# Attention and soft mixture of experts on one core: when the expert weights are loaded during attention

## The chip, the cores and the metric

One core of a Trainium2 chip. Times are microseconds on the device, from the first to the last instruction of a run of the whole program. A run is one launch; the time of a kernel is the median of its runs.

## What is computed

All data is float32. First comes attention over 8 batches of 12 heads, 448 positions and 64 channels, with a sigmoid in place of a softmax. Its output, as 3584 rows of 768, goes through a soft mixture of 8 experts with 4 slots each.

```python
scores = scale * np.matmul(q, k.transpose(0, 1, 3, 2)) - np.log(S)
x = np.matmul(1.0 / (1.0 + np.exp(-scores)), v)      # then laid out as 3584 x 768
logits = x @ phi                                     # 3584 x 32
slot_input = softmax(logits, axis=0).T @ x           # over all rows: 32 x 768
for e in range(8):                                   # 4 slots of each expert
    h = np.maximum(slot_input[e] @ w1[e], 0.0)       # w1[e]: 768 x 1024
    slot_out[e] = h @ w2[e]                          # w2[e]: 1024 x 768
return softmax(logits, axis=1) @ slot_out
```

The softmax over rows runs over all batches, so the experts can't start before attention is done; their weights (w1 and w2, 50 MB) can be loaded before.

## The kernel before

**Attention** runs in 24 rounds (the loop over n), three to a batch (NQ = 3). A round takes four heads as two pairs, pa and pb. Its work on TensorE: the scores of both pairs (`qk_full`, L170), their products with V (`av_full`, L188), the logits of the round before (`logits`, L217), and what the 448 positions leave over beyond three blocks of 128 (`qk_mid` L181, `av_mid` L197). ScalarE takes the sigmoids (L160). VectorE brings the output of the round before out of PSUM (`evac`, L206), transposes it (`turn`, L212) and splits the queries and keys of the next round in two parts (`split_all`, L149 and L151).

**The slot job.** From the second batch on, a round also holds a share of the mixture for the batch before, bp. Three flags name the rounds: *edge* is the first round of a batch (n = 3, 6, ...), *after* the second (n = 4, 7, ... 22) and *third* the third. In an edge round the last logits come in and the running softmax begins (`softmax_a`, `softmax_b`). In the after round VectorE finishes it (`softmax_r`, `softmax_c`) and `spread` (L281) spreads the weights of the slots: a transpose on VectorE (L283), a write to a scratch buffer in DRAM (zd, L285), and four reads back, each to another quarter of the partitions (dr, L288). The slot job of TensorE (`slot_mm`, L309, 112 matmuls) reads dr; it stands in the after round behind the logits. VectorE adds its result up in the third round (L331).

**Loads.** All DMAs are issued by SyncE's queue (SP), in the order of the program text; an entry that waits holds up those behind it. At the top of a round stand the queries and keys of the next round (`load_qk`, L134, two buffers), which wait until this round's are no longer read; in an after round then the five DMAs of `spread`; then V of the next round (`load_v`, L141, two buffers); then weights (`load_unit`, L92).

**Weights** are cut into 128 units of 384 KB, 64 of w1 and 64 of w2, loaded in that order into a ring of 47 buffers (N_A, names wa) and 21 more (N_B, names wb). The first 47 have memory of their own during attention. The loop at L432 brings their number up to (n + 1) * 47 // 21 in round n: 2 units in most rounds, 3 in some, and all 47 by round 20. The 21 take over memory of attention's buffers, so their loads wait until those are read for the last time. The other 60 are loaded as buffers come free.

**After attention** come the last batch's slot job, the experts' first layer (L519), the second in two halves of the columns (L584), and the combination (L562), whose results are copied to ring buffers and stored.

Order of instructions on TensorE, SyncE, VectorE and ScalarE is that of the program text; buffers, waits and semaphores come from the tile framework.

Of the kernel before, what the change touches and what calls it, by code (L numbers as in the profile page):

```python
# [16 lines left out]
B, H, S, D = 8, 12, 448, 64  # L17
# [5 lines left out]
NQ = NPR // 2  # L23
# [4 lines left out]
N_A = 47  # L28
# [19 lines left out]
def soft_moe_attention(ctx: ExitStack, tc: tile.TileContext, qk, v, phi, w1, w2, cst, out):  # L48
# [25 lines left out]
    state = {"next": 0, "ring": 0, "wpb": None}  # L74
# [10 lines left out]
    def load_unit():  # L85
        n = state["next"]
        if n >= len(units):
            return
        state["next"] = n + 1
        u = units[n]  # L90
        t = ring_tile()[:]
        nc.sync.dma_start(t, w1[u[1:]] if u[0] == "w1" else w2[u[1:]])  # L92
        utile[u] = t
# [9 lines left out]
    def combine_d(b, cb):  # L103
        lt = lt_all[:, b].rearrange("p (j s) -> p j s", j=NBK)
        cz = small.tile([P, NBK, 1], F32, name="cz")
        nc.vector.tensor_reduce(out=cz[:], in_=lt, axis=AX.X, op=ALU.add)
        nc.vector.tensor_scalar(cz[:], cz[:], 1e-9, None, op0=ALU.add)
        nc.vector.reciprocal(cz[:], cz[:])
        nc.vector.tensor_tensor(
            out=cb.rearrange("p (j s) -> p j s", j=NBK), in0=lt, in1=cz.broadcast_to([P, NBK, NSLOT]), op=ALU.mult)  # L110
        nc.vector.transpose(lt_all[:, b], cb)
# [4 lines left out]
    with ExitStack() as actx:  # L116
# [9 lines left out]
        def bank2(i):  # L126
            return ps.tile([P, 2, 512], F32, name=f"b{i}")
# [3 lines left out]
        def load_qk(p):  # L131
            if p < NP:
                t = ldq.tile([P, QW], F32, name="qkt")
                nc.sync.dma_start(t[:], qk[p])  # L134
                qkts[p] = t

        def load_v(n):
            if n == NG:
                return
            vs[n] = lvp.tile([P, 2 * NFULL + 1, P], F32, name="v")  # L140
            nc.sync.dma_start(vs[n][:], v[n])  # L141
# [11 lines left out]
        def split_all(p):  # L153
            if p < NP:
                for i, z in ((0, 0), (0, 1), (1, 0), (1, 1)):
                    split(p, i, z)
# [6 lines left out]
        def qk_full(p):  # L163
            qs, ks = splits[p, 0], splits[p, 1]
            for c in range(NFULL):
                u = p % 2 * NFULL + c
                sc = bank2(u % 4)
                for z, y in ((0, 0), (0, 1), (1, 0)):
                    for h, r in enumerate(heads):
                        nc.tensor.matmul(  # L170
                            sc[:, h, 0:S], ks[r, z, c * P:(c + 1) * P], qs[r, y, :], start=(z + y == 0), stop=(z == 1))
                atts[p, c] = sigmoid(f"att{u % NATT}", sc)
# [31 lines left out]
        def evac(n):  # L204
            new_x(n)
            nc.vector.tensor_copy(xTs[n][:], avs[n][:, :, 0:S])  # L206

        def turn(p):
            b, hp = divmod(p, NPR)
            if hp == 0:  # L210
                ys[b] = xp.tile([P, NPR, S], F32, name="y")
            nc.vector.transpose(ys[b][:, hp, :], xTs["p", p])  # L212
# [17 lines left out]
        def logits(n, i):  # L230
            lp = bank2(i)[:, 0, :]
            logits_job(lp, (2 * n, 2 * n + 1))
            return lp
# [21 lines left out]
        def softmax_r(b):  # L255
            zt, pe = dts[b][:, 0, :], dts[b][:, 1, :]
            n = P if b == 0 else P + 1
            nc.vector.reciprocal(zt[:, 0:n], zt[:, 0:n])
            nc.vector.tensor_tensor(out=pe[:, 0:n], in0=pe[:, 0:n], in1=zt[:, 0:n], op=ALU.mult)

        def softmax_c(b):
            pe = dts[b][:, 1, :]
            if b == 0:
                nc.vector.tensor_reduce(out=mz[:, 1:2], in_=pe[:, 0:P], axis=AX.X, op=ALU.add)
            else:
                zb = small.tile([P, 1], F32, name="zb")
                nc.vector.tensor_reduce(out=zb[:], in_=pe[:, 0:P], axis=AX.X, op=ALU.add)
                nc.vector.scalar_tensor_tensor(
                    out=mz[:, 1:2], in0=mz[:, 1:2], scalar=pe[:, P:P + 1], in1=zb[:], op0=ALU.mult, op1=ALU.add)
# [6 lines left out]
        def combine_c(b):  # L276
            neg = dts[b][:, 1, 0:P]
            nc.vector.reciprocal(neg, neg)
            nc.vector.tensor_tensor(out=lt_all[:, b], in0=lt_all[:, b], in1=neg, op=ALU.mult)

        def spread(b):  # L281
            z = dts[b][:, 0, 0:P]
            nc.vector.transpose(z, dts[b][:, 1, 0:P])  # L283
            flat = bounce.tile([P, P], F32, name="zd")
            nc.sync.dma_start(flat[:], z)  # L285
            drs[b] = xp.tile([P, 4, NBK * BLK], F32, name="dr")
            for a in range(4):
                nc.sync.dma_start(drs[b][32 * a:32 * a + 32, :, :], flat[:].rearrange("(j i) n -> i j n", j=4))  # L288
# [37 lines left out]
        def slot_evac(b):  # L326
            for a in range(4):
                if b == 0:
                    nc.vector.tensor_copy(acc_of[:, a], new_of(slots[b], a))
                else:  # L330
                    nc.vector.scalar_tensor_tensor(  # L331
                        out=acc_of[:, a], in0=acc_of[:, a], scalar=dts[b][:, 1, P:P + 1], in1=new_of(slots[b], a),
                        op0=ALU.mult, op1=ALU.add)
# [80 lines left out]
        for n in range(NG):  # L414
            pa, pb = 2 * n, 2 * n + 1
            bp = n // NQ - 1
            edge, after, third = (n >= NQ and n % NQ == i for i in range(3))
            final = n == NG - 1
            load_qk(pa + 2)
            load_qk(pb + 2)  # L420
            if third:
                slot_evac(bp)
            if n > 0:
                evac(n - 1)
                for p in ((pa - 4, pa - 3) if third else ()) + (() if after else (pa - 2, pa - 1)):
                    turn(p)
            if after:
                softmax_r(bp)
                softmax_c(bp)
                spread(bp)  # L430
            load_v(n + 1)
            while state["next"] < min(N_A, (n + 1) * N_A // 21):  # L432
                load_unit()
            if third:
                combine_c(bp)
            if edge and bp > 0 or final:
                bq = bp if final else bp - 1
                combine_d(bq, dts[bq][:, 0, 0:P])
            qk_full(pa)
            split_all(pa + 2)  # L440
            qk_full(pb)
            split_all(pb + 2)
            if final:
                avs["p", pa] = bank2(2)[:, 0, :]
                av_full(pa, True, False)
                lg = bank2(0)[:, 0, 0:P]
                nc.tensor.matmul(lg, ident, lt_all[:, B - 1], start=True, stop=False)
                logits_job(lg, [NP - 4, NP - 3], first=False, last=False)
                avs["p", pb] = bank2(3)[:, 0, :]
                av_mid(n, ((False, True), (True, False)))  # L450
                xa = xp.tile([P, 2, S], F32, name="xT", bufs=2)[:, 0, :]
                xTs["p", pa] = xa
                nc.vector.tensor_copy(xa, avs["p", pa][:, 0:S])
                turn(pa)
                av_full(pb, False, True)
                logits_job(lg, [pa], first=False, last=False)
                xb = xp.tile([P, 2, S], F32, name="xT", bufs=2)[:, 0, :]
                xTs["p", pb] = xb
                nc.scalar.copy(xb[:, 256:S], avs["p", pb][:, 256:S])
                nc.vector.tensor_copy(xb[:, 0:256], avs["p", pb][:, 0:256])  # L460
                logits_job(lg, [pb], first=False)
                turn(pb)
                break
            avs[n] = bank2(2)
            for i in range(2):
                avs["p", pa + i] = avs[n][:, i, :]
            av_full(pa, True, False)
            if edge:
                lp = logits(n - 1, 0)
                logits_add(lp, bp, False)  # L470
                softmax_a(bp)
                softmax_b(bp)
            av_full(pb, True, False)
            if n > 0 and not edge:
                lp = logits(n - 1, 3 if after else 0)
                if after:
                    combine_b(bp)
                logits_add(lp, n // NQ, n % NQ == 1)
            if after:
                slot_job(bp)  # L480
            qk_mid(n + 1)
            av_mid(n, ((False, True), (False, True)))
# [179 lines left out]
```

## Time and profile before

| | |
|---|---|
| median of 3 runs | 395.81 us (393.76 to 398.99) |
| the profiled execution | 397.69 us, span 395.9 us, clock 0.98 |
| TensorE busy | 370.6 us (94%) |
| VectorE, ScalarE busy | 227.4 us, 188.1 us |
| moved by DMA | 97.52 MB, mean 246 GB/s |
| weight units loaded | 92 to wa buffers, 36 to wb buffers |

The profile is that of one execution. PE is TensorE's matmuls, PEld its weight loads, which run beside them, DVE VectorE, ACT ScalarE, and SPq the issuing of DMAs by SyncE. A row of SP's queue gives the start and the length of issuing, not of the transfer. "Idle <- X" names what ended an engine's wait. "issue" is a wait for nothing that the profile shows. Queue q1 holds the data, queues q8 and q14 hold instructions. A line of forty digits gives the busy share in tenths over forty equal slices of the time asked for.

### The profile page before, as it was taken

To read this page: it belongs to the slowest core of one execution; us is meant where nothing else is said; L and a number is where in the kernel's file an instruction comes from. 1 tells how busy PE (TensorE), PEld (TensorE's weight loads), DVE (VectorE), ACT (ScalarE), POOL (GpSimd) and SP (SyncE) were. 2 spreads that over 40 slices of the span, in tenths; PEclk is the share of its full clock that TensorE was granted. 3 is DMA by queue.
4 is the path that set the end of the run, shared out by engine and by line. 5 is a ranking of instruction groups with operands and counts; after the bars stand their busy time and mean duration, and the time that the engine had idled before them with its cause. 6 is when DMAs were issued, how large, how long until landed. Compare 5 with 4: busy or idle time off the path is not lost.

```text
span 395.9 us, 9573 instructions
## 1 busy us (share of the span) xinstructions
PE 370.6 (94%) x4000; PEld 192.9 (49%) x4000; DVE 227.4 (57%) x531; ACT 188.1 (48%) x244; POOL 3.4 (1%) x13
## 2 busy tenths in 40 slices
PE   8999999999999999989999999999989989988760
PEld 6445556554455654455554455555465544314220
DVE  3555677776787767677767778775531420330250
ACT  4656676564667556466645666663520110230240
POOL 1000000000000000000000000000020000000000
PEclk9999999999999999999999999999997999999995
DMA  6555658645665846565376558523899999999997
GB/s 215 213 191 202 220 172 285 202 168 170 252 220 145 299 154 225 165 221 210 110 237 215 189 176 284 190 101 124 304 365 351 403 400 401 390 376 406 365 301 238
DMA packets 41851, 97.52 MB, mean 246 GB/s; under 512 B 4304, under 2 KB 16208, under 8 KB 41808
## 3 DMA queue, kind: packets, MB, share of 16 engines
q1 hardware_dynamic: 41808, 96.91, 69.5%
q8 instruction: 31, 0.51, 0.5%
q14 instruction: 12, 0.10, 0.1%
HBM read 85.43 MB, written 11.47 MB: 245 GB/s over the span
## 4 chain that ended last, share of the span: by engine, by line
PE 84%; DMA 8%; DVE 2%; issue 1%; ACT 1%; SPq 1%; ACTq 0%
PE b L188 27%; PE b L170 23%; PE px L519 6%; PE b L181 6%; PE b L197 5%; PE b L309 4%; PE po L584 4%; DMA wb<-in_w_dram 4%; PE b L217 3%; PE px L562 3%; DMA out_dram<-wb 2%; DMA qkt<-in_qk_dram 1%; PE px L536 1%; DMA zd<-t 1%; PE b L376 1%
## 5 line engine op out<-in xcount | busy, mean ns | idle before, releaser
L160 ACT ACTIVATE att<-b,nbias 128x896 f32<-128x896 f32 x144 | 132.0, 1016 | 14.9 <-PE b L170 14.9
L188 PE MATMUL b<-att,v 128*64 128x448 f32 x576 | 115.3, 545 | 0.0
L170 PE MATMUL b<-qs,ks 64*128 64x448 f32 x864 | 96.3, 372 | 0.5 <-issue 0.5
L170 PEld LDWEIGHTS b<-qs,ks 64*128 64x128 f32 x864 | 77.7, 184 | 26.9 <-PE b L181 15.5
L188 PEld LDWEIGHTS b<-att,v 128*64 128x64 f32 x576 | 38.5, 136 | 61.6 <-issue 49.9
L160 ACT ACTIVATE attm<-b,nbias 128x896 f32<-128x896 f32 x24 | 24.2, 1008 | 72.1 <-PE b L181 72.1
L206 DVE COPY xT<-b 128x896 f32<-128x896 f32 x23 | 25.1, 1092 | 34.5 <-PE b L197 34.5
L151 DVE TENSOR_TENSOR qs<-qkt,qs 128x448 fp32r<-128x448 f32 x48 | 30.0, 625 | 1.7
L151 DVE TENSOR_TENSOR ks<-qkt,ks 128x384 fp32r<-128x384 f32 x48 | 26.8, 558 | 1.6
L212 DVE STREAM_TRANSPOSE y<-xT 128x448 f32<-128x448 f32 x48 | 27.3, 617 | 0.4
L181 PE MATMUL b<-qkt 64*64 64x448 f32 x192 | 24.5, 562 | 0.6 <-DMA qkt<-in_qk_dram 0.6
L197 PE MATMUL b<-attm,v 64*64 64x448 f32 x192 | 22.5, 538 | 1.8 <-issue 1.8
L149 DVE CAST qs<-qkt 128x448 fp32r<-128x448 f32 x48 | 18.2, 379 | 7.3 <-DMA qkt<-in_qk_dram 7.0
L519 PE MATMUL px<-wa,sT 128*32 128x256 f32 x282 | 19.2, 422 | 0.9 <-DVE sT L380 0.9
L567 DVE COPY wa<-px 96x768 f32<-96x768 f32 x13 | 12.2, 952 | 12.3 <-PE px L562 12.3
L562 PE MATMUL px<-st,lt_all 32*96 32x384 f32 (+1 forms) x128 | 17.0, 524 | 1.5 <-DVE st L597 0.7
L567 ACT COPY wa<-px 128x768 f32<-128x768 f32 x13 | 10.3, 800 | 16.8 <-PE px L562 16.7
L309 PE MATMUL b<-y,dr 32*32 32x192 f32 x896 | 17.8, 331 | 0.4 <-DMA dr<-zd 0.3
L217 PEld LDWEIGHTS b<-xT,phit 128*32 128x32 f32 x384 | 9.1, 109 | 17.0 <-issue 13.4
L149 DVE CAST ks<-qkt 128x384 fp32r<-128x384 f32 x47 | 16.6, 353 | 0.0
L217 PE MATMUL b<-xT,phit 128*32 128x96 f32 (+1 forms) x384 | 16.0, 266 | 0.2
L597 DVE COPY st<-px 128x384 f32<-128x384 f32 x2 | 1.1, 558 | 25.5 <-PE px L595 25.5
(132 smaller groups left out, 235.5 us busy)
## 6 DMA issues: line engine op xcount, KB each, us to landing
wa<-in_w_dram SPq DMA_DIRECT2D x92, 384.0 KB, 7.2
qkt<-in_qk_dram SPq DMA_DIRECT2D x48, 448.0 KB, 3.7
wb<-in_w_dram SPq DMA_DIRECT2D x36, 384.0 KB, 6.6
v<-in_v_dram SPq DMA_DIRECT2D x24, 448.0 KB, 5.5
out_dram<-wa SPq DMA_DIRECT2D x13, 384.0 KB, 5.1
out_dram<-wa SPq DMA_DIRECT2D x13, 288.0 KB, 5.3
dr<-zd SPq DMA_DIRECT2D x28, 64.0 KB, 2.0
out_dram<-wb SPq DMA_DIRECT2D x3, 384.0 KB, 8.1
```

The source lines that it names most:

```text
L149: copy(dst[:, 0, :], src)
L151: nc.vector.tensor_tensor(out=dst[:, 1, :], in0=src, in1=dst[:, 0, :].bitcast(F32), op=ALU.subtract)
L160: nc.scalar.activation(att[:], sc[:, :, 0:S], AF.Sigmoid, bias=nbias, scale=QSCALE)
L170: nc.tensor.matmul(sc[:, h, 0:S], ks[r, z, c * P:(c + 1) * P], qs[r, y, :], start=(z + y == 0), stop=(z == 1))
L181: nc.tensor.matmul(sc[r, h, 0:S], t[d, S + NQK:QW], t[d, 0:S], start=True, stop=True)
L188: nc.tensor.matmul(avs["p", p][r, 0:S], vs[n][:, i * (NFULL + 1) + c, r], atts[p, c][:, h, :], start=(start and c == 0), stop=(stop and c ...
L197: nc.tensor.matmul(avs["p", 2 * n + i][d, 0:S], vt[r, NFULL, d], att[r, h, :], start=start, stop=stop)
L212: nc.vector.transpose(ys[b][:, hp, :], xTs["p", p])
L217: nc.tensor.matmul(lp[32 * j:32 * j + 32, 0:TOK[j]], phi_sb[:, p % NPR, :], xTs["p", p][:, TOF[j]:TOF[j] + TOK[j]], start=(first and m == ...
L309: nc.tensor.matmul(sl[a // 2][32 * j:32 * j + 32, a % 2, 0:NPR * BLK], drs[b][32 * a:32 * a + 32, j, c * BLK:(c + 1) * BLK], y[32 * a:32 * ...
L519: nc.tensor.matmul(ph[32 * j:32 * j + 32, uu, 0:256], sT[:, 3 * kh + kc, :], utile[("w1", e, 2 * uu + j // 2, kh)][:, kc * 256:(kc + 1) * ...
L562: nc.tensor.matmul(pf[j // 2][0:TOK[j], j % 2, 0:HALF], lt_all[r, b, 0:TOK[j]], st[r, :], start=True, stop=True)
```

## The change

In each round V of the next round is now loaded straight behind the queries and keys, ahead of `spread`. And units of weights are loaded in the first round of each batch only (n = 0, 3, ... 18), up to (n // 3 + 1) * 47 // 7: 6, 7, 7, 6, 7, 7 and 7 units. All 47 are in by round 18. The order on the other engines, the buffers and their number stay.

```diff
             if after:
                 softmax_r(bp)
                 softmax_c(bp)
+            load_v(n + 1)
+            if after:
                 spread(bp)
-            load_v(n + 1)
-            while state["next"] < min(N_A, (n + 1) * N_A // 21):
+            while n % NQ == 0 and state["next"] < min(N_A, (n // NQ + 1) * N_A // (B - 1)):
                 load_unit()
             if third:
                 combine_c(bp)
```

## The prediction

> **What bounds the kernel now.** I read the page first, then busy time by stretches, the waits of TensorE, the chain of waits around the longest of them, SP's own queue, and the DMA traffic round by round. From the page, the totals, the forty slices, the instruction queue and the issue of weights:
>
> ```profile
> span 395.9 us, 9573 instructions
> PE 370.6 (94%) x4000; PEld 192.9 (49%) x4000; DVE 227.4 (57%) x531; ACT 188.1 (48%) x244; POOL 3.4 (1%) x13
> ...
> DMA  6555658645665846565376558523899999999997
> ...
> q8 instruction: 31, 0.51, 0.5%
> ...
> wa<-in_w_dram SPq DMA_DIRECT2D x92, 384.0 KB, 7.2
> ```
>
> Two stretches with different limits show in the DMA line, and the busy time by stretches (length; busy us of each engine; clock; DMA share; GB/s) gives them figures:
>
> ```profile
> 97.00:275.00 178.00, 175.41 (x1952) 94.12 (x1944) 129.77 (x318) 104.26 (x126) 0.00 (x0) 1.00 0.57 193
> 275.00:380.00 105.00, 97.27 (x1080) 45.58 (x1076) 33.78 (x70) 25.56 (x50) 2.24 (x8) 0.97 0.99 370
> ```
>
> Up to 275 us the DMA engines are 57% busy and TensorE is busy 175.4 of 178 us: attention is bound by TensorE. After it the DMA engines are 99% busy: what is left is 81 units of weights and the output, and that stretch lasts as long as its bytes. It begins when TensorE lets go of the last ring buffers; SP's queue issues the 21 units of the second ring from there:
>
> ```profile
> 274.51 22.84 SPq L92 DMA_DIRECT2D wb<-in_w_dram  x21
> ```
>
> The change leaves the bytes after 274.5 us as they are (47 units are in before it either way, by round 18 in place of 20). So a microsecond that TensorE saves or loses before 274.5 us moves the end by about a microsecond, and nothing else counts. What TensorE waited for in 0 to 290 us, all but its start and one wait of 0.6 us for the first queries:
>
> ```profile
> PE b L197 <- issue: 1.8, 1, 1.8
> ...
> PE b L170 <- issue: 0.5, 1, 0.5
> PE b L309 <- DMA dr<-zd: 0.3, 1, 0.3
> ```
>
> That is the whole stock from which a gain can come: 2.6 us, 0.7% of the span.
>
> **The two waits with no releaser.** In the chain of waits (start, length, what) the shorter one stands behind round 10's slot job and the longer just behind round 13's; the second fence is that slot job by itself, in the timeline of TensorE:
>
> ```profile
> 133.16 0.48 issue
> ...
> 166.77 0.91 PE b L181 x8
> 167.68 1.80 issue
> 169.48 0.98 PE b L197 x8
> ```
> ```profile
> 164.57 2.19 PE L309 MATMUL b<-y,dr 32*32 32x192 f32 x112
> ```
>
> TensorE waited for no engine and no DMA. The page has 31 packets on the instruction queue of some 16 KB, and TensorE runs 4000 matmuls and 4000 weight loads: 258 instructions to a packet. A round without a slot job has 92 pairs, 184 instructions in 11.0 us (143.73 to 154.73 in SP's rows below); the slot job alone has 112 pairs, 224 instructions in 2.19 us. It is the one place where TensorE runs through nearly a block of instructions in 2 us. In the DMA view of 0.2 us at 167 us, and in that of 131.3 to 131.5 us, ahead of the shorter wait, one packet stands each time:
>
> ```profile
> q8 instruction: 1, 0.02, 30.6%
> ```
> ```profile
> q8 instruction: 1, 0.02, 28.8%
> ```
>
> They begin at 167.0 and 131.4 us; TensorE goes on 2.4 and 2.2 us later. So the next block was fetched only 2.5 us after the slot job began. What was ahead of it is in SP's queue, rounds 12 (its start) and 13:
>
> ```profile
> 143.73 0.82 SPq L134 DMA_DIRECT2D qkt<-in_qk_dram  x2
> 144.66 0.37 SPq L141 DMA_DIRECT2D v<-in_v_dram  x1
> 145.07 1.40 SPq L92 DMA_DIRECT2D wa<-in_w_dram  x3
> 154.73 0.82 SPq L134 DMA_DIRECT2D qkt<-in_qk_dram  x2
> 158.64 0.33 SPq L285 DMA_DIRECT2D zd<-t  x1
> 160.19 1.75 SPq L288 DMA_DIRECT2D dr<-zd  x4
> 162.04 0.37 SPq L141 DMA_DIRECT2D v<-in_v_dram  x1
> 162.46 0.91 SPq L92 DMA_DIRECT2D wa<-in_w_dram  x2
> ```
>
> V and two units, 1.2 MB, were issued at 162.0 to 163.4 us, and were still under way at 167. I read the wait as the fetch standing behind them.
>
> **The change part by part.** *Removed from the rounds that hold a slot job (n = 4, 7, ... 19) and from those after them:* two to three units in each; and V, which stays, moves 7.3 us forward in its round (from 162.04 to just behind the queries, as in round 12, where it is issued 0.93 us after the round's first load). Then nothing is in flight when the slot job starts. If the packet begins 0.5 us after the slot job's start (chosen between 0 and the 2.5 seen), the block is there at 164.57 + 0.5 + 2.4 = 167.5, ahead of 167.68: both waits go, **-2.28 us** (1.80 + 0.48). The bounds are 0 (the packet takes its 2.5 us all the same) and -2.28.
>
> *Added to rounds 0, 3, ... 18:* a burst of 6, 7, 7, 6, 7, 7, 7 units behind queries and V. SP needs 0.45 us for each issue; nothing is queued behind them but the next round's loads, 11 us later. The bytes do not fit. Round 12's three units, in the DMA line of 143 to 155 us (0.3 us a slice), keep the engines at it until 152.6 us:
>
> ```profile
> DMA  0000077359999999897917999999996410000000
> ```
>
> Each further unit costs 1.09 us (22.84 / 21, above): four more end at 157.0. Round 13's queries are issued at 154.73 and would have begun to move near 155.6. So they are **1.4 us late**. The split of queries on VectorE would wait for them a little; it has cover, since in that round VectorE waits for TensorE afterwards:
>
> ```profile
> 129.02 0.56 DVE L226 COPY lt_all<-b 64x128 f32<-64x128 f32 x2 [1.55 <-PE b L217]
> ```
>
> I price that at nothing; without the 1.55 us of cover it would be up to 1.4 us in five rounds.
>
> *Moved:* V ahead of the slot weights' DRAM write (zd). SP passes no wait by this: V's buffer comes free with the last product of the round before, and zd waits for VectorE until 3.9 us into the round anyway (154.73 to 158.64). On the DMA engines it counts, though: zd now stands behind V. Round 21 has queries and V and no unit, and its DMA line (250 to 261 us, 0.275 us a slice) ends at 255.5, 5.4 us after its first issue at 250.05, with SP held up for 0.8 us at V; so V ends 4.6 to 5.4 us into a round:
>
> ```profile
> 250.05 0.82 SPq L134 DMA_DIRECT2D qkt<-in_qk_dram  x2
> 250.91 1.21 SPq L141 DMA_DIRECT2D v<-in_v_dram  x1
> ```
> ```profile
> DMA  0029757999999979996100000000000000000000
> ```
>
> The landing times in round 13 (154 to 167 us):
>
> ```profile
> dr<-zd SPq DMA_DIRECT2D x4, 64.0 KB, 2.0
> zd<-t SPq DMA_DIRECT2D x1, 64.0 KB, 1.5
> ```
>
> zd lands 5.45 us into the round. Behind V alone it lands 0 to 0.5 us later; with the burst's 1.4 us ahead of both, 1.0 to 1.9 us later. The four reads (dr) and the slot job follow it. Their slack: the fourth read is issued at 160.19 + 1.75 - 0.43 = 161.5 and lands at 163.5, against a slot job at 164.57, 1.06 us. Another 0.45 us is hidden, because the job starts on the first three reads. Round 22 shows this, where zd took twice as long and the job broke off after 24 of its matmuls:
>
> ```profile
> zd<-t SPq DMA_DIRECT2D x1, 64.0 KB, 3.1
> ```
> ```profile
> 270.85 0.67 PE L309 MATMUL b<-y,dr 32*32 32x192 f32 x24
> 271.83 1.74 PE L309 MATMUL b<-y,dr 32*32 32x192 f32 x88 [0.31 <-DMA dr<-zd]
> ```
>
> It ran 2.72 us for 2.19, a loss of 0.53 us for a fourth read that landed about a microsecond after the job's start. So 1.5 us of slack stand against 1.0 to 1.9 us of lateness: a loss of 0 to 0.4 us in each of the five rounds behind seven units, 0 in the two behind six. I take 0.1, **+0.5 us** together (0 to 2.0). Round 22 has no burst ahead; its 0.53 us stays (0 to 1.0).
>
> *Sum:* 395.9 - 2.28 + 0.5 = 394.1 us of span. The profiled execution took 397.69 us, 1.8 more than its span and 1.9 more than the median of 395.81; taking the same 1.8 us off the median gives **394.0 us**. The runs themselves lie between 393.76 and 398.99, so 2% (7.9 us) is about what a measurement of this kernel can tell from no change.
>
> **The rivals.** *The backlog does not hold the fetch.* Then the two waits have another cause, they stay, and only the costs come: 395.8 + 0.5 = 396.3 us. For it speaks that rounds 4, 7 and 16 load units in the same place without such a wait; against it, that both waits have a packet 2.2 to 2.4 us ahead of their end, and that the two stand at different places (L197 and L170), as the end of a block would that shifts from batch to batch. The Trainium skill (DMA: Bandwidth & Descriptors, Queues, rings and completion order) has each DMA engine take turns between its queue rows packet by packet. By that rule a fetch would pass the backlog and this rival holds; the 2.5 us at round 13 speak against it, but the trace does not record when the fetch was asked for.
>
> *The DRAM bounce becomes the bound (slower).* zd takes 1.5 us more wherever it meets other traffic, as in round 22, on top of the 1.4 us of burst: late by 2.8, less 1.5 of slack, 1.3 us in five rounds, 0.3 in round 10, 0.7 more in round 22, 7.5 together; less 2.28, it is +5.2, **401.0 us**. It decides when zd lands later than 6.95 us into its round (5.45 + 1.5). For it: the overlap above. Against: round 22's delay went with an instruction packet at that moment, not with data.
>
> *More is won.* Both waits go, no slot job is late and round 22's 0.53 us goes too, because in the runs timed such waits are longer than in the profiled one (the slowest is 3.2 us above the median): 395.8 - 2.8 = 393.0, and down to 391.5 if the timed runs had a microsecond or more of them besides.
>
> **How the numbers follow.** Forecast 0.5 (392.8 to 395.6), no hold of the fetch 0.2, the bounce 0.18, more won 0.12. The range takes the forecast, all of the first rival, the lower part of the bounce and most of the last: 391.5 to 399.5. Faster by over 2% would need 387.9 and no stock is that large: 0.03. Slower by over 2% needs 403.7, a bounce 2 us worse in every batch than I price it: 0.05. Within 2%: 0.92.
>
> **What would show it.** Right: TensorE's waits without a releaser behind rounds 10 and 13 are gone, V stands in SP's queue ahead of zd, the second ring's first unit is issued near 272.7, and DMA traffic runs without a gap from each burst into the next round. Wrong: waits of the slot job for dr in most batches with zd landing 7 us into the round (the bounce), or waits of about 2 us without a releaser in other rounds (the fetch is not held by what I say). It is also wrong if the end does not follow the first issue of the second ring.

## The result and the profile after

The changed kernel takes 397.89 us (median of 22 runs, 394.41 to 402.13), the kernel before 395.98 us (22 runs beside them): a ratio of 1.0059, with a 95% interval of 1.0036 to 1.0082. A second series gave 1.0037 (1.0001 to 1.0073). It is slower by some 2 us, where 2 us less was forecast. Medians here and below are over all runs; ratios leave out runs more than 1.5% above the fastest of their kernel. The profiled execution took 399.63 us, span 397.9.

TensorE's waits in 0 to 290 us, complete, in the changed kernel:

```profile
PE b L404 <- DVE nbias L69: 1.2, 1, 1.2
PE b L309 <- DMA dr<-zd: 0.8, 2, 0.6
```

Both waits without a releaser are gone, as forecast. In their place stand waits of the slot job (L309) for dr. The 0.8 us are only the part in which TensorE stood still; the rest shows in how long the job takes. In the timeline of TensorE it takes 3.24 us in round 4 and 2.93 us in round 7, where it took 2.19 before:

```profile
59.05 3.24 PE L309 MATMUL b<-y,dr 32*32 32x192 f32 x112 [0.20 <-DMA dr<-zd]
...
94.93 2.93 PE L309 MATMUL b<-y,dr 32*32 32x192 f32 x112
```

SP's queue at the start of rounds 12 and 13, and the second ring's first issue:

```profile
144.45 0.82 SPq L134 DMA_DIRECT2D qkt<-in_qk_dram  x2
145.37 0.38 SPq L141 DMA_DIRECT2D v<-in_v_dram  x1
145.80 3.88 SPq L92 DMA_DIRECT2D wa<-in_w_dram  x7
155.46 0.80 SPq L134 DMA_DIRECT2D qkt<-in_qk_dram  x2
156.35 0.38 SPq L141 DMA_DIRECT2D v<-in_v_dram  x1
159.37 0.33 SPq L285 DMA_DIRECT2D zd<-t  x1
162.39 2.71 SPq L288 DMA_DIRECT2D dr<-zd  x4
...
274.97 22.79 SPq L92 DMA_DIRECT2D wb<-in_w_dram  x21
```

zd is issued 3.9 us into the round as before, but lands at 162.4, 3.0 us later, where it took 1.5. The DMA view of round 13's first 10 us (0.25 us a slice; kind, count, KB, us to landing) shows what is ahead of it: the burst from the round before, queries and V fill the engines to 5.5 us, with stragglers to 6.2.

```profile
DMA  9997795689899989999885100000000181635100
...
q8 instruction: 1, 0.02, 0.7%
...
qkt<-in_qk_dram SPq DMA_DIRECT2D x2, 448.0 KB, 4.8
v<-in_v_dram SPq DMA_DIRECT2D x1, 448.0 KB, 5.8
dr<-zd SPq DMA_DIRECT2D x4, 64.0 KB, 3.1
zd<-t SPq DMA_DIRECT2D x1, 64.0 KB, 3.0
```

V, issued at 156.35, landed at 162.15, and zd 0.2 us behind it. In this round that was not all: zd was 1.5 us late, which is just the slack, but the four reads took 3.1 us in the median, where they took 2.0 before. An instruction packet was moved in the same 10 us; that it held the reads up is not shown.

Round by round, from the first load of one to the first load of the next, for round 22 to the second ring's first issue (from SP's queue; two profiles of the changed kernel):

| round | 4 | 7 | 10 | 13 | 16 | 19 | 22 | 11 | 14 |
|---|---|---|---|---|---|---|---|---|---|
| before, us | 12.98 | 12.94 | 12.94 | 12.98 | 12.95 | 12.98 | 13.50 | 11.69 | 12.82 |
| changed | 14.29 | 13.71 | 12.98 | 13.87 | 13.63 | 13.52 | 12.98 | 10.85 | 10.82 |
| changed, second | 12.98 | 16.49 | 12.95 | 14.88 | 14.03 | 12.99 | 12.98 | 10.80 | 10.82 |
| zd to landing, changed | 4.57 | 3.51 | 2.54 | 3.00 | 3.27 | 3.43 | 3.08 | | |
| zd to landing, second | 3.04 | 4.97 | 2.41 | 3.62 | 3.45 | 2.68 | 3.14 | | |

So 4.2 us were lost in rounds 4 to 19 in the first profile and 6.6 in the second, and 3.4 us won in rounds 11, 14 and 22 (11.69 + 12.82 + 13.50 less 10.85 + 10.82 + 12.98). Round 10, behind six units, lost nothing.

### The profile page after: what moved, and what is told of

It reads as the page before. It is cut to its first block, busy times and chain, and to the rows that moved or that the text cites. A ratio compares the mean times of both kernels' runs of the same rounds, so it can differ in the third digit from the quotient of the medians.

```text
span 397.9 us, 9565 instructions
## 1 busy us (share of the span) xinstructions
PE 371.3 (93%) x4000; PEld 193.0 (49%) x4000; DVE 228.0 (57%) x531; ACT 188.0 (47%) x244; POOL 3.4 (1%) x13
## 4 chain that ended last, share of the span: by engine, by line
PE 79%; DMA 12%; DVE 3%; issue 1%; ACT 1%; SPq 0%; ACTq 0%
PE b L188 25%; PE b L170 21%; PE px L520 6%; PE b L181 6%; PE b L309 5%; PE b L197 5%; PE po L585 4%; DMA wb<-in_w_dram 3%; PE b L217 3%; DMA zd<-t 3%; PE px L563 2%; DMA dr<-zd 2%; DMA out_dram<-wb 2%; DMA out_dram<-wa 2%; PE px L537 1%
## 5 line engine op out<-in xcount | busy, mean ns | idle before, releaser
L309 PE MATMUL b<-y,dr 32*32 32x192 f32 x896 | 20.4, 332 | 1.3 <-DMA dr<-zd 0.8
L520 PE MATMUL px<-wa,sT 128*32 128x256 f32 x282 | 18.1, 404 | 0.9 <-DVE sT L380 0.9
L309 PEld LDWEIGHTS b<-y,dr 32*32 32x32 f32 x896 | 13.1, 103 | 7.3 <-issue 2.7
```

The source lines that it names most:

```text
L309: nc.tensor.matmul(sl[a // 2][32 * j:32 * j + 32, a % 2, 0:NPR * BLK], drs[b][32 * a:32 * a + 32, j, c * BLK:(c + 1) * BLK], y[32 * a:32 * ...
L520: nc.tensor.matmul(ph[32 * j:32 * j + 32, uu, 0:256], sT[:, 3 * kh + kc, :], utile[("w1", e, 2 * uu + j // 2, kh)][:, kc * 256:(kc + 1) * ...
```

## The experiments

**The theory**: the slot job waits for the DRAM bounce, which the burst and V hold up; what is won is the fetch of instructions. **Rivals**: one part of the change does it alone; the place is the end of the program; the waits without a releaser have nothing to do with bytes in flight. Ratios are to the kernel before, of the same series, with 95% intervals.

**V ahead alone** (v_ahead), the lines of the units as before:

```diff
-                spread(bp)
             load_v(n + 1)
+            if after:
+                spread(bp)
```

> V ahead of the write of the slot weights, units placed as before. Theory (the write stands behind V's bytes, and behind the burst's in the changed kernel): zd lands 0 to 0.8 us later than its 1.5 us, inside 1.5 us of slack, so the slot jobs lose 0 to 0.2 us each, and two units in place of V and two units stand ahead of the instruction fetch: 395 to 396 us, zd at 1.6 to 2.3 us. Rival (V's place alone costs what the changed kernel lost): zd at 3 us or more in most rounds with a slot job and about 398 us.

Measured 0.9997 (0.9966 to 1.0028). zd landed after 1.9 to 2.6 us in rounds 4 to 19; these rounds lasted 12.97 to 13.00 us. Round 13's first 10 us:

```profile
DMA  0009924699999999999971000004435545793568
...
zd<-t SPq DMA_DIRECT2D x1, 64.0 KB, 1.9
```

The engines begin at 0.75 us and are done at 5.5. V's place alone costs 0.4 to 1.1 us of zd here and nothing of the time. Rounds 11 and 14 were 11.20 and 12.31 us, in between, with less ahead of the fetch.

**The burst alone** (burst):

```diff
-            while state["next"] < min(N_A, (n + 1) * N_A // 21):
+            while n % NQ == 0 and state["next"] < min(N_A, (n // NQ + 1) * N_A // (B - 1)):
```

> Units in the first round of a batch only, V behind the reads as before. Theory (V and the burst add up ahead of the write): the burst alone makes zd 1 to 1.5 us later, about what the slack covers, so 0 to 0.3 us in each of five slot jobs, and the two waits for the instruction fetch shrink: 394 to 396 us. Rival (the burst alone does it): zd at 3 to 4.5 us as in the changed kernel, 0.5 to 1.3 us lost in five slot jobs, 397 to 398 us.

Measured 1.0011 (0.9980 to 1.0043). zd landed after 1.5 to 2.8 us; of rounds 4 to 19 only 13 and 16 were longer, by 0.2 and 0.1 us. Round 13:

```profile
DMA  9999999679899998643831100000000626262789
...
zd<-t SPq DMA_DIRECT2D x1, 64.0 KB, 2.8
```

The burst runs into the round and queries follow it, but they are done some 1.3 us earlier than with V. Neither part alone has the loss: each eats most of the slack, and only together do they exceed it by much. A wait without a releaser was left in each, of 1.2 us in v_ahead and of 0.4 us here, both in round 13.

**The changed kernel again** (after2), no edit.

> The changed kernel once more. Its first profile lost 4.2 us at six slot jobs (0.5 to 1.3 us each, zd landing 2.5 to 4.6 us after its issue). Theory (that loss is steady): zd again at 2.5 to 4.6 us and rounds 4, 7, 13, 16 and 19 again 0.5 to 1.3 us longer than 12.95 us; 1.5 to 3 us slower than before. Rival (the loss at the slot jobs is chance and the difference lies in the final stores): the rounds differ and the stretch of the last stores is again 30 us in place of 28.

Measured 1.0037 (1.0001 to 1.0073). The loss is steady in kind, not in place: 3.5 us in round 7, none in rounds 4 and 19. The rival is half right: the rounds differ, and the stretch of the last stores was again long (30.1 us, for 30.3 in the first profile and 27.9 before).

**The slot job without the bounce** (no_bounce): on the changed kernel, the weights of the first seven slot jobs come from a constant tile, so what these jobs add up is not the slots' input; all DMAs stay.

```diff
-                            drs[b][32 * a:32 * a + 32, j, c * BLK:(c + 1) * BLK],
+                            csb[32 * a:32 * a + 32, c * BLK:(c + 1) * BLK] if const
+                            else drs[b][32 * a:32 * a + 32, j, c * BLK:(c + 1) * BLK],
```

> The changed kernel, but the slot jobs of the first seven batches take their weights from the constant tile that is loaded at the start, in place of dr, so they use wrong weights and wait for no DMA; zd and dr are still moved. Theory (what the change loses is the slot job's wait for dr, and what it wins is the fetch): all slot rounds last 12.95 us, no wait without a releaser over 0.5 us, the time is 393.5 to 395.5 us, 2 to 4 us under the changed kernel. Rival (a part of the loss has another cause): 396.5 us or more.

Measured 392.93 us, 0.9915 (0.9883 to 0.9947). zd was as late as in the changed kernel (3.1 us in round 13, 4.8 in round 19), and yet all seven slot rounds lasted 12.94 to 12.98 us. Its complete waits of TensorE up to 290 us:

```profile
PE b L405 <- DVE nbias L69: 1.2, 1, 1.2
```

This settles the loss. From 1.0037 or 1.0059 down to 0.9915 is 4.8 to 5.7 us, give or take some 2 us by the intervals: that is what waiting for dr costs the changed kernel. And 0.85%, 3.4 us (2.1 to 4.6), is what is won without it, of which some 0.5 us is round 22's wait. That is more than none_in_after wins (below), which has no wait without a releaser either; the difference was not explained.

**More slack, by another order** (after_mid_first):

```diff
+            qk_mid(n + 1)
             if after:
                 slot_job(bp)
-            qk_mid(n + 1)
```

> The changed kernel with the scores of the leftover positions (8 matmul pairs, 0.91 us) moved ahead of the slot job, so the job starts 0.9 us later against dr while the DMAs stay as they are. Theory (the loss is the slot job's wait for dr): 0.9 us of each wait is covered by other work, 3 to 3.8 us come back, about 394 to 395 us. Rival (the loss comes from elsewhere, such as traffic that slows the engines): no change from 397.9 us.

Measured 402.19 us, 1.0148 (1.0097 to 1.0200), far from both forecasts. No wait for dr is left, but the edit brought waits of its own:

```profile
PE b L181 <- PE b L217: 4.9, 7, 0.7
```

The leftover scores take the PSUM bank of the logits and now follow them directly. A pair of rounds lost 1.0 to 1.7 us, of which 0.7 are this wait; the rest I put down to the scores of the next round, which come straight behind the sums that free the slot job's banks, but that is not shown. It tells nothing of the theory; no_bounce does what it was meant for.

**zd on a queue of its own** (zd_on_act): the changed kernel with that write issued by ScalarE, called behind `qk_full(pa)`.

```diff
-            nc.sync.dma_start(flat[:], z)
+            nc.scalar.dma_start(flat[:], z)
```

> The changed kernel with the write of the slot weights issued by ScalarE behind its first three sigmoids of the round, so it doesn't share a queue with V and the burst. Theory A (it waits in its queue behind V's bytes): zd lands 1.5 to 2 us after its issue, which is some 0.4 us later in the round than on SP; the slot jobs lose 0 to 0.3 us and the time is 394.5 to 396 us. Theory B (it is the DMA engines that are busy, whatever the queue): zd still needs 2.5 to 4.5 us and the time stays at 397 to 399 us.

Measured 397.08 us, 1.0025 (0.9994 to 1.0056): at the lower edge of B's range, but not told apart from no change. The view of DMA issues decides for B:

```profile
zd<-t ACTq DMA_DIRECT2D x7, 64.0 KB, 3.3
```

A median of 3.3 us on its own queue, against 3.3 and 3.1 us on SP's. The write is issued at the same point of the round; it never took over 3.7 us, and rounds 4 to 19 lost 1.8 us together, less than in the changed kernel, but it waits all the same. In round 13 V was issued at 154.27 and landed 6.3 us later, the write was issued at 157.29 and landed 3.4 us later: it came right behind V, as on SP's queue. The Trainium skill (DMA: Bandwidth & Descriptors, Queues, rings and completion order) has each engine take turns between queues, packet by packet. By that rule I would have expected the write to land ahead of V, and it didn't; how its bytes lay between V's on each engine the views do not show.

**All units in the round of the slot job** (all_in_after), behind the reads:

```diff
+            while n % NQ == 1 and state["next"] < min(N_A, (n // NQ + 1) * N_A // 7):
```

> The kernel before with all units of a batch, six or seven, in the round of the slot job, behind the reads; V behind them as before. zd and dr have nothing ahead of them. Theory (TensorE's fetch of instructions waits behind the bytes in flight): the waits without a releaser at the slot jobs of rounds 10 and 13 grow from 0.5 to 2.3 us to 2 to 6 us and others appear; 398 to 404 us. Rival (they don't depend on the bytes ahead): they stay at 0.5 to 2.3 us, 395 to 397 us.

Measured 406.08 us (400.15 to 412.84), ratio 1.0144 (1.0066 to 1.0222): slower, but by how much is uncertain. The waits without a releaser grew and came behind three slot jobs in place of two:

```profile
66.51 2.09 PE L170 MATMUL b<-qs,ks 64*128 64x448 f32 x18 [1.79 <-issue]
102.54 4.56 PE L170 MATMUL b<-qs,ks 64*128 64x448 f32 x27 [1.85 <-issue]
140.51 5.47 PE L170 MATMUL b<-qs,ks 64*128 64x448 f32 x35 [2.13 <-issue]
```

Rounds 5, 8 and 11 lasted 12.87, 14.51 and 14.89 us for 10.8; in the last two TensorE's clock fell as well (last section). The instruction packets ahead of these last two waits began 4.7 and 4.1 us after the start of the slot job, for 2.5 us in the kernel before. Bytes behind the reads do hold TensorE up. A further 2.3 us of waits, in rounds 15, 18 and 21, are for VectorE; that the queries behind such a burst make it late is an argument, not shown.

**The kernel before, again** (before2) and **with four warm-up matmuls less** (warm4, `WARM = 4`).

> The kernel before, once more, for its profile. If the two waits without a releaser come from where blocks of instructions end in the program, they stand again behind the slot jobs of rounds 10 and 13, 0.3 to 2 us long; if they are chance, they stand elsewhere or are missing. The part from the second ring's first unit to the end was 121.4 us before and 122.9 us changed; if that difference is chance, this run may show either.

> The kernel before with four of the eight warm-up matmuls at its start left out, which takes 16 instructions from the head of TensorE's program and nothing else. Theory (the waits stand where a block of instructions ends): all block ends move 16 instructions later in the program, the shift from one batch to the next is 17 the other way, so the pattern moves on by one batch: the short wait at the first scores behind the slot job comes in round 13's place and the long one ahead of the leftover products in round 16's. Rival (the waits belong to the traffic of rounds 10 and 13): they stay there.

before2 had its waits in the same two places, 1.1 and 2.3 us long. warm4 had them one batch on, behind the slot jobs of rounds 13 and 16:

```profile
167.71 3.92 PE L170 MATMUL b<-qs,ks 64*128 64x448 f32 x36 [1.43 <-issue]
204.16 0.53 PE L181 MATMUL b<-qkt 64*64 64x448 f32 x1 [2.41 <-issue]
```

Sixteen instructions fewer at the head moved a wait 35 us away, within one matmul of where it was expected. It is the fetch of the next block of instructions, where the block's end falls behind a slot job.

**No units in the slot's round, V behind the reads** (none_in_after, twice), **and the same with V ahead** (spread_v):

```diff
+            while n % NQ != 1 and state["next"] < min(N_A, (2 * (n // NQ) + 1 + n % NQ // 2) * N_A // 14):
```

> No units in the rounds with a slot job; three or four in each of the two other rounds of a batch; V behind the reads as before. Theory: no burst reaches the next round, zd lands in 1.5 us as before, only V stands ahead of the instruction fetch, so the two waits without a releaser go (2.3 us) and the time is 393 to 394.5 us. Rival (the fetch isn't held by the units): the waits stay and the time is 396 us. Second rival (what was lost lies in the part after attention): 397 to 398 us, with the second ring's first unit issued earlier than before.

> The kernel with no units in the rounds of the slot job and V behind the reads, once more, to narrow its interval: its first ratio was 0.9965 (0.9926 to 1.0005). Theory (the waits for instructions are gone, and they cost the kernel before 1 to 2 us on average): 0.994 to 0.998. Rival (those waits are an affair of single runs and worth nothing on average): 0.999 to 1.002.

> No units in the rounds with a slot job, three or four in the two others, and V ahead of the write as in the changed kernel. Theory (V alone makes zd 0.4 to 1.1 us later, within the slack, and nothing is in flight when the slot job starts): no slot round over 13.0 us but round 22 (13.5), no wait without a releaser, 393.5 to 395.5 us. Rival (V ahead costs by itself): slot rounds 0.3 us or more longer and 396 us or more.

none_in_after: 0.9965 (0.9926 to 1.0005) and 0.9987 (0.9958 to 1.0017). All waits without a releaser are gone, the instruction packets at the slot jobs of rounds 10 and 13 begin 1.1 and 0.5 us after the job's start in place of 2.5, zd lands in 1.5 us in rounds 4 to 19, and rounds 1 to 22 took 254.9 and 255.0 us, for 257.6 and 259.6 in the two profiles of before. It is the fastest of the versions that keep all the work, and faster than the changed kernel; from the kernel before it isn't clearly told apart. spread_v: 0.9999 (0.9964 to 1.0035). V ahead cost 0.7 us in each of rounds 7 and 19, where zd landed after 3.7 us though three units at most were loaded in the round ahead. That was not expected. The queries landed late there too (4.4 and 4.3 us in the median, for 3.6 to 3.9 in the other slot rounds); why is open. A wait of 0.2 us without a releaser was left.

**What stays open.** In none_in_after, 2.6 to 4.7 us less in the rounds came out as 0.5 to 1.4 us of time. v_ahead and burst show the same: 256.9 and 255.4 us in these rounds, and no gain in time. In both its profiles the part from the second ring's first unit to the end took 123.1 us, for 121.4 and 120.5 before; the last loads are issued at about the same distance, and the stores take longer. That part varied between 120.5 and 123.9 us over all profiles, and why wasn't settled. Both profiled executions of before (397.7 us) also lie above the medians of their series, by 1.7 and 2.8 us, so its waits for instructions may be shorter in the mean than those shown. The two of the changed kernel lie 1.7 and 3.0 us above, so the same may hold for its losses.

## Why the prediction was wrong

- **The stock and the place**: right. What was won lay in the waits named, 3.4 us in their three rounds for a stock of 2.6, and the bound was TensorE up to 275 us.
- **-2.28 us for the two waits**: right in its cause (warm4, all_in_after, none_in_after) and in that both go. The rival that the backlog doesn't hold the fetch has fallen. What the two waits gave was 2.8 us in the profile (rounds 11 and 14). In the timed runs it lies between the 0.5 to 1.4 us of none_in_after and the 2.9 us of no_bounce without round 22, and isn't settled.
- **The burst's overrun, 1.4 us**: right for round 13, where the queries took 4.8 us to land for 3.5 before, but too small and too even. Over the ten rounds behind seven units in the two profiles they were 1.7 us late in the mean, and from 0.8 to 3.4.
- **+0.5 us for the slot jobs**: the step that failed. It set a lateness of zd of 1.0 to 1.9 us against 1.5 us of slack and took 0.1 us a round. The slack was right: round 4 of the second profile, 1.5 us late, lost nothing. But behind seven units zd was 1.2 to 3.5 us late, 2.0 in the mean of ten rounds, and the loss was 4.2 and 6.6 us in the profiles, 4.8 to 5.7 us in the timed runs (no_bounce). The mechanism was the rival's, the bounce, which had a chance of 0.18, 7.5 us of loss and 401.0 us; it came out at two thirds to three quarters of that loss.
- **Why it was mis-sized**: the estimate took V and the burst as bytes at the mean rate, and the end of that stream as sharp. V alone made zd 0.7 us late in the mean of five rounds (v_ahead), the burst alone 0.7 (burst), both 2.0. zd and each read are done when their slowest part is, and the engines end unevenly: I read the "5 1", "4 3 2 1" behind the nines in the DMA lines as such stragglers. A mean also hides what counts here, since only what goes beyond the slack is lost: by zd alone that is 2.6 and 2.9 us in the two profiles. The rest had no term: reads that were late as well (round 13), and in the second profile a halved clock (last section).
- **Round 22**: taken as unchanged, it lost its 0.5 us of waiting although zd still took 3.1 us; it is counted in the 3.4 us won.
- **"Where the end follows the second ring's first issue"**: only roughly. That issue came 0.46 us later than before (4.2 lost, 3.4 won, 0.4 less in the other rounds), the end of the profiled execution 2.0 us later; the rest lies in the last stores, whose spread of a microsecond or two the sum had no term for.

## What to carry to other kernels

A small transfer with a deadline is priced by what is in flight on the DMA engines when it is issued, not by its own size; two changes that each leave it inside its slack can break it together. Before concentrating loads in one place, add up the bytes up to the next small transfer and, going by the figures of this case, leave as much again for the engines' uneven ends. And look for stretches where an engine runs through its instructions quickly: the fetch of the next block also stands behind the loads.

## What the runs showed of the hardware

TensorE's clock fell to half in the middle of the work, for 3.41 us, after the waits of the slot job in round 7 of after2. The rows are the stretch ahead, that stretch and the one behind (with length; busy us of PE, PEld, DVE, ACT, POOL; granted clock; DMA share; GB/s):

```profile
93.05:96.46 3.41, 2.41 (x87) 1.21 (x90) 1.81 (x6) 0.62 (x2) 0.00 (x0) 1.00 0.29 82
96.46:99.87 3.41, 3.41 (x67) 1.65 (x48) 1.39 (x4) 0.04 (x1) 0.00 (x0) 0.50 0.00 0
99.87:103.28 3.41, 3.41 (x34) 2.39 (x28) 2.58 (x4) 2.78 (x4) 0.00 (x0) 1.00 0.68 226
```

In the stretch ahead TensorE was idle for 1.0 us. Half the clock for 3.41 us is worth up to 1.7 us, as an estimate; with the 1.9 us by which zd, 3.4 us late, went beyond the slack, that accounts for the 3.5 us lost there. The Trainium skill (TensorE: Matmul & The Clock Gate, Part 1: The HAM clock gate) has the clock at half after an idle window of about 3.4 us; here 1.0 us of idle time within 3.41 us was enough.

The clock fell in the same way behind waits without a releaser, so these too can cost more than their length. In before2 it was 0.50 from 169.10 to 172.51 us, behind the wait of 2.3 us, and round 14 was 4.0 us longer than a round without a wait. In all_in_after it was 0.50 from 103.23 and from 140.78 us, behind the second and third wait. In these three cases TensorE had been idle for 1.9 to 2.1 us of the 3.41 us ahead. Idle time alone doesn't decide it: in warm4 it was idle for 1.4 us between 165.43 and 168.84 us, and the clock stayed at 1.00.
